# Query-key stacks tiled by kind instead of by token half, and the product with V split only at PSUM banks

## The chip, the cores and the metric

One core of one Trainium2 chip. The time is device microseconds of one execution, median over runs; the kernel is one program launched once, with everything from the first LayerNorm to the last store inside.

## The reference

S = 2048 tokens, D = 640, 32 heads of 20, window W = 256, gMLP width Fh = 864:

```python
def _A_ref(x, wqkv, wo):
    q, k, v = ...                      # (x @ wqkv) as 32 heads of 20
    scores = einsum("bhqd,bhkd->bhqk", q, k) * 20 ** -0.5
    mask = (i - j >= 0) & (i - j < 256)
    p = softmax(where(mask, scores, -1e9))
    return einsum("bhqk,bhkd->bhqd", p, v) ... @ wo

def _B_ref(x, w_in, w_sp, b_sp, w_out):
    z = gelu(x @ w_in)
    z1, z2 = z[..., :Fh], layernorm(z[..., Fh:])
    g = einsum("ts,bsf->btf", w_sp, z2) + b_sp
    return (z1 * g) @ w_out

h = x + _A_ref(layernorm(x), wqkv, wo)
out = h + _B_ref(layernorm(h), w_in, w_sp, b_sp, w_out)
```

## The kernel before

**Stages.** LayerNorm of x and the V projection, then the query and key projections (line 568 to 570), then attention, then the output projection with the residual, then the gMLP. The instruction order of TensorE (PE), VectorE (DVE), ScalarE (ACT) and SyncE (SP) is the order in which the code is written; each of these engines works strictly in that order, and an instruction that waits holds back all behind it on its engine. GpSimd (POOL) is placed by the scheduler.

**Precision by parts.** A query or key is cut into three bf16 parts. A dot product of 20 numbers becomes one matmul of 120 rows: six pairs of parts times 20. Rows 120 to 122 hold, for queries, three parts of minus the row's maximum, and for keys the constant ONES, so that a matmul over 123 rows gives score minus maximum, ready for the exponential.

**Stacks.** Four heads at a time form a stack g (8 stacks). A stack lies in one of three slots, `slot_0`, `slot_1` and the pair `xb`; the next but one is loaded while one is in use. Every slot has two SBUF tiles. Before, tile b holds one half of the tokens (0 to 1023, 1024 to 2047), and in it queries (a = 0) and keys (a = 1) of the four heads. `load_stack` fills it with 24 DMAs (L311) out of the DRAM buffer `qk_d`: for each half of the tokens six pairs of parts, each for queries and for keys. SP issues them in the attention steps, one or two to a step, the first half of the tokens first; the last is issued about at the end of the stack two ahead.

**Steps.** The attention stage is a loop over 128 steps s; step s belongs to stack g = s // 16 and to its block of keys kb = s % 16 of 128 tokens. Each step has four turns hh, one for a head. A turn issues

- `max_item(s + 16, hh)`: the query block one stack ahead against its up to 384 keys, in four matmuls of 32 query rows and 288 keys (L341; while the lead is built up, one matmul of 128 rows, L345), into one of three banks; then the masked row maximum on DVE (L351);
- `score_item(s, hh)`: the key block against up to 384 queries, four matmuls of 32 key rows and 288 queries (L394; in the last 15 steps the sixteen of two heads share a double bank), into one of three other banks; then the exponential on ACT (L397) into `pt`; after the fourth turn POOL puts zeros outside the window;
- at turn 1 and at turn 3 one of the two parts of `pv_item(s - 2)`, the product of V with the 384 exponentials of a key block (L422), four matmuls, one for each head, accumulated into a bank `pv` that stands for 512 queries. A part ends at column 512 where the block crosses a bank; where none ends inside, the 384 columns are cut into 192 and 192.

When an odd block kb is done, 256 queries are complete and are copied out of the bank: the first half of a bank by ACT (L438), the second by DVE; L441 stores them.

**The maxima's way.** After eight query blocks, at turn 1 of the step with (s + 16) % 8 == 0, `max_rows` transposes the 32 columns of maxima (L357), DVE and POOL make three parts, L366 stores them to the DRAM buffer `m_d`, and one step later L368 loads them into rows 120 to 122 of the queries of the right token half. So the second half's maxima of a stack (b = 1) are written in the first steps of that same stack, eight steps before a score needs them.

**Where a matmul's tokens cross from one tile to the other** (at token 1024) `tokens` cuts it into two.

Of the kernel before, what the change touches and what calls it, by code (L numbers as in the profile page):

```python
# [7 lines left out]
F32 = mybir.dt.float32  # L8
F32R = mybir.dt.float32r
BF16 = mybir.dt.bfloat16  # L10
# [5 lines left out]
P = 128  # L16
S = 2048
D = 640
H = 32
DH = 20  # L20
# [8 lines left out]
ONES = 1.0019378662109375  # L29
# [5 lines left out]
def block_kernel(ctx, tc, x, xt, wqk, wv, wo, w_in, wsp, bsp, w_out, out):  # L35
    nc = tc.nc
# [201 lines left out]
    with ExitStack() as ab:  # L238
# [59 lines left out]
        def load_stack(g):  # L298


            st = slot_w[g % 3]
            if g < 3:
                for h in st:
                    nc.gpsimd.memset(h[96:P, 1], ONES)
                    if g == 2:
                        yield
            for b in range(2):
                for j, parts in enumerate(((0, 0), (0, 1), (0, 2), (1, 0), (1, 1), (2, 0))):
                    for a in range(2):
                        src = qk_d[g // 4, parts[a], b, a * DH:(a + 1) * DH, g % 4 * 4:g % 4 * 4 + 4]  # L310
                        nc.sync.dma_start(st[b][j:6 * DH:6, a], src)  # L311
                        yield

        def tokens(st, rows, a, hh, t0, n):

            o = 0
            while o < n:
                c, t = divmod(t0 + o, S // 2)
                w = min(n - o, S // 2 - t)
                yield o, w, st[c][:rows, a, hh, t:t + w]  # L320
                o += w

        def one(st, rows, a, hh, t0, n):
            (_, _, x), = tokens(st, rows, a, hh, t0, n)
            return x

        def max_item(g, qb, hh, strips=True):

            st = slot_ap[g % 3]
            ps = s1_tile()  # L330
            lo = max(0, qb - 2) * P
            n = (qb + 1) * P - lo
            keep = mask[:, 384 - n:]
            if strips:
                skip = 32 if qb > 1 else 0
                if skip:
                    n, keep = 288, strip
                for j in range(4):
                    q0 = qb * P + 32 * j
                    for o, w, k in tokens(st, 120, 1, hh, lo + skip * j, n):  # L340
                        nc.tensor.matmul(ps[32 * j:32 * j + 32, o:o + w], one(st, 120, 0, hh, q0, 32), k,  # L341
                                         start=True, stop=True, tile_position=(0, 32 * j))
            else:
                for o, w, k in tokens(st, 120, 1, hh, lo, n):
                    nc.tensor.matmul(ps[:, o:o + w], one(st, 120, 0, hh, qb * P, P), k, start=True, stop=True)  # L345
            b, c = divmod(qb, 8)
            if c == 0 and hh == 0:
                m_cols[g, b] = tmp2.tile([P, 32], F32, tag="mcol", bufs=2, name=f"mcol{g}_{b}")
            junk = tmp2.tile([P, 384], BF16, tag="junk", bufs=2, name=f"junk{g}_{qb}_{hh}")
            c += hh * 8  # L350
            nc.vector.tensor_tensor_reduce(out=junk[:, :n], in0=ps[:, :n], in1=keep, scale=1.0,  # L351
                                           scalar=NEG, op0=OP.add, op1=OP.max, accum_out=m_cols[g, b][:, c:c + 1])

        def max_rows(g, b):

            ps = s1_tile()[:32, :P]
            nc.tensor.transpose(ps, m_cols.pop((g, b)), ident)  # L357
# [8 lines left out]
            nc.sync.dma_start(rows.rearrange("a r c -> r a c"), m3.bitcast(F32))  # L366
            yield
            nc.sync.dma_start(slot_w[g % 3][b][120:123, 0], rows.rearrange("a (h r) c -> a h (r c)", h=4))  # L368
            yield

        p_tiles, pv_tiles = {}, {}
# [1 line left out]
        def score_item(u, hh):  # L373


            g, kb = divmod(u, NT)
            st = slot_ap[g % 3]
            n = min(384, S - kb * P)
            if hh == 0:
                p_tiles[u] = tmp3.tile([P, 4, 384], F32, tag="pt", bufs=4, name=f"pt{u}")  # L380
            pt = p_tiles[u]
            if u > NU - LEAD:
                if hh % 2 == 0:
                    bank2.append(bank2.pop(0))
                ps = bank2[-1][:, hh % 2]
            else:
                ps = s2_tile()
            for i in range(4):
                k0 = kb * P + 32 * i
                b, e = 32 * i, min(n, 32 * i + 288)  # L390
                if NU - LEAD < u and 4 * (u - NU + LEAD - 1) + hh < 6:
                    b, e = 0, n
                for o, w, q in tokens(st, 123, 0, hh, kb * P + b, e - b):
                    nc.tensor.matmul(ps[32 * i:32 * i + 32, b + o:b + o + w], one(st, 123, 1, hh, k0, 32), q,  # L394
                                     start=True, stop=True, tile_position=(0, 32 * i))
            if u <= NU - LEAD:
                nc.scalar.activation(pt[:, hh, :n], ps[:, :n], AF.Exp, scale=SCALE)  # L397
# [46 lines left out]
        if True:  # L444
# [134 lines left out]
            def split_qk(m, c, ps):  # L579
                sg = tmp.tile([P, 3, 512], BF16, tag="ta", bufs=3, name=f"sg{m}_{c}")  # L580
                rest = tmp.tile([P, 512], F32, tag="tb", bufs=2, name=f"rest{m}_{c}")
                nc.vector.tensor_tensor(out=rest, in0=ps, in1=stds[c], op=OP.mult)
                yield
                nc.scalar.activation(sg[:, 0, :], rest, AF.Copy)
                yield
                (nc.gpsimd if m > 5 else nc.vector).tensor_tensor(out=rest, in0=rest, in1=sg[:, 0, :],
                                                                  op=OP.subtract)
                if (m, c) == (9, 3):
                    nc.gpsimd.tensor_copy(out=sg[:, 1, :], in_=rest)
                else:  # L590
                    nc.scalar.activation(sg[:, 1, :], rest, AF.Copy)
                nc.gpsimd.tensor_tensor(out=sg[:, 2, :], in0=rest, in1=sg[:, 1, :], op=OP.subtract)
                T = S // 4
                base = qk_d[m // 5, 0, c // 2, m % 5 * 8, 0, c % 2 * 256:c % 2 * 256 + 256]
                nc.sync.dma_start(bass.AP(tensor=base.tensor, offset=base.offset,
                                          ap=[[T, P], [2 * 2 * DH * H // 2 * T, 3], [1, 256]]), sg.bitcast(F32))

            halves = [slice(0, HD), slice(HD, D)]
            load_x(0)
# [807 lines left out]
```

## Time and profile before

| | |
|---|---|
| median of 3 runs | 1126.63 us (1126.02 to 1129.81) |
| profiled execution | 1125.76 us, span 1124.0 us |
| mean granted TensorE clock | 0.995 |
| busy, share of the span | PE 97%, weight loads 87%, DVE 67%, ACT 50%, POOL 28% |
| attention steps 0 to 111 | about 239 to 449 us |

PE is busy for 1089.4 us of 1124.0. In the rows below, a line of a timeline gives the start in us, the time in us until the last of the group ends (or of one, for a single instruction), the engine, the code line, the operation and its output and inputs, partitions by free size, and after x the number of instructions; what stands in brackets is the idle time just before and what ended it. Rows of stages give the stretch, its length, then busy time with the number of instructions for PE, weight loads, DVE, ACT and POOL, then the granted clock, the share of DMA engines that are busy and GB/s. SPq is the queue of DMA issues on SP.

### The profile page before, as it was taken

What the parts mean: (1) busy time and instruction counts of PE and PEld (TensorE: products, weight loads), DVE (VectorE), ACT (ScalarE), POOL (GpSimd) and SP (SyncE); (2) the same over time, 40 slices, a digit from 0 to 9 for tenths busy, and PEclk for the clock granted to TensorE, in tenths of its full rate; (3) what the DMA queues carried; (4) which work ended last, traced back from release to release, by engine and by line L of the source; (5) the groups of instructions that cost most, each with busy time, mean ns of one, the idle gap of its engine ahead of it and who ended that gap; (6) DMA issues with size and microseconds to landing.
All of it is one profiled execution on the core that took longest, in us unless ns stands there. A gap on an engine that the chain in (4) does not pass through costs nothing.

```text
span 1124.0 us, 28713 instructions
## 1 busy us (share of the span) xinstructions
PE 1089.4 (97%) x11139; PEld 980.3 (87%) x11139; DVE 752.8 (67%) x2070; ACT 567.5 (50%) x1155; POOL 319.6 (28%) x447
## 2 busy tenths in 40 slices
PE   8999999989999999999999999999999999999998
PEld 8998887657877777699899999999999899999998
DVE  6643444779988999588877678655358974556542
ACT  4444443248988899735566567434347521222210
POOL 4324446766766666723200011000001000000000
PEclk9999999989999999999999999999999999999999
DMA  7834567545555555689554522242251563444321
GB/s 256 283 113 135 171 186 248 183 157 181 179 179 172 177 178 165 170 249 311 218 195 167 182 91 76 75 134 90 104 171 57 180 209 119 124 148 148 98 87 60
DMA packets 87672, 180.57 MB, mean 161 GB/s; under 512 B 11440, under 2 KB 45760, under 8 KB 83648
## 3 DMA queue, kind: packets, MB, share of 16 engines
q1 hardware_dynamic: 87536, 178.74, 49.8%
q8 instruction: 87, 1.43, 0.5%
q14 instruction: 49, 0.40, 0.1%
HBM read 120.82 MB, written 57.88 MB: 159 GB/s over the span
## 4 chain that ended last, share of the span: by engine, by line
PE 72%; DMA 8%; ACT 7%; DVE 6%; issue 3%; POOL 2%; SPq 1%; DVEq 0%; POOLq 0%; ACTq 0%
PE g L1136 22%; PE out_ps L1201 8%; ACT pt L397 5%; PE pv L422 4%; PE zb L1028 4%; PE qk L568 3%; PE qk L569 3%; PE qk L570 3%; PE bank L341 3%; PE bank L394 3%; PE zx L976 2%; PE zv L976 2%; PE zy L976 1%; PE wo_ps L101 1%; DMA o_d<-ot 1%
## 5 line engine op out<-in xcount | busy, mean ns | idle before, releaser
L397 ACT ACTIVATE pt<-bank 128x384 f32<-128x384 f32 (+1 forms) x452 | 180.1, 478 | 26.4 <-PE bank L394 16.2
L803 ACT ACTIVATE aw<-fx 128x512 fp32r<-128x512 f32 (+2 forms) x160 | 93.7, 596 | 173.5 <-PE g L1136 120.7
L1136 PE MATMUL g<-zl,aw 128*128 128x432 f32 x768 | 171.0, 358 | 0.0
L351 DVE CUSTOM_DVE_ANT_0 junk<-bank,strip 128x288 bf16<-128x288 f32 x392 | 156.7, 454 | 16.3 <-PE bank L341 13.8
L1136 PEld LDWEIGHTS g<-zl,aw 128*128 128x128 f32 x768 | 143.6, 188 | 5.9
L422 PE MATMUL pv<-pt,v_sb 128*32 128x192 f32 (+3 forms) x1984 | 129.6, 323 | 6.2 <-ACT ot L438 3.8
L1136 PE MATMUL g<-ze,aw 128*128 128x432 f32 x576 | 134.0, 360 | 0.3 <-DVE row L797 0.2
L797 DVE TENSOR_TENSOR aw<-fx,aw 128x512 fp32r<-128x512 f32 (+2 forms) x160 | 102.7, 647 | 37.1 <-ACT aw L803 35.8
L1136 PEld LDWEIGHTS g<-ze,aw 128*128 128x128 f32 x576 | 107.0, 188 | 6.7 <-ACT aw L803 1.2
L401 POOL TENSOR_SCALAR_AFFINE_SELECT pt<-pt 128x512 f32<-128x512 f32 x128 | 83.9, 656 | 62.7 <-ACT pt L397 60.2
L394 PE MATMUL bank<-slot 123*32 123x288 bf16 (+7 forms) x1296 | 94.4, 276 | 4.9 <-ACT pt L397 3.5
L1201 PE MATMUL out_ps<-wout,y_sp 128*128 128x320 f32 (+1 forms) x630 | 96.2, 309 | 0.4 <-ACT y_sp L140 0.4
L341 PE MATMUL bank<-slot 120*32 120x288 bf16 (+6 forms) x1280 | 92.2, 277 | 3.6 <-issue 1.6
L1028 PE MATMUL zb<-win,aw 128*128 128x432 f32 x480 | 95.4, 359 | 0.0
L1201 PEld LDWEIGHTS out_ps<-wout,y_sp 128*128 128x128 f32 (+1 forms) x630 | 94.1, 188 | 1.2 <-ACT y_sp L140 0.7
L87 POOL TENSOR_TENSOR mvz<-mvz,half 128x1 f32<-128x1 f32 x16 | 10.1, 633 | 298.8 <-DVE mvz L86 296.8
L1028 PEld LDWEIGHTS zb<-win,aw 128*128 128x128 f32 x480 | 89.9, 187 | 5.0 <-ACT row L803 0.3
L422 PEld LDWEIGHTS pv<-pt,v_sb 128*32 128x32 f32 x1984 | 59.9, 110 | 18.1 <-issue 9.9
L797 DVE TENSOR_TENSOR row<-g,row 128x432 f32<-128x432 f32 x80 | 48.2, 604 | 37.8 <-PE g L1136 36.9
L394 PEld LDWEIGHTS <-slot 123*32 123x32 bf16 x1728 | 58.5, 97 | 15.3 <-issue 6.0
L404 POOL TENSOR_SCALAR_AFFINE_SELECT pt<-pt 128x512 f32<-128x512 f32 x112 | 71.4, 637 | 0.0
L351 DVE CUSTOM_DVE_ANT_0 junk<-bank,mask 128x384 bf16<-128x384 f32 (+2 forms) x120 | 51.7, 447 | 21.1 <-PE bank L345 15.8
(196 smaller groups left out, 2247.1 us busy)
## 6 DMA issues: line engine op xcount, KB each, us to landing
slot<-qk_d SPq DMA_DIRECT2D x144, 160.0 KB
fx<-wsp_in SPq DMA_DIRECT2D x32, 512.0 KB
qk_d<-sg SPq DMA_DIRECT2D x40, 384.0 KB
fx<-hn_d SPq DMA_DIRECT2D x32, 320.0 KB
o_d<-ot SPq DMA_DIRECT2D x64, 128.0 KB
xb<-qk_d SPq DMA_DIRECT2D x48, 160.0 KB
z_d<-row SPq DMA_DIRECT2D x16, 432.0 KB
g_d<-row SPq DMA_DIRECT2D x16, 432.0 KB
```

Of the source, the lines that this page charges most:

```text
L341: nc.tensor.matmul(ps[32 * j:32 * j + 32, o:o + w], one(st, 120, 0, hh, q0, 32), k, start=True, stop=True, tile_position=(0, 32 * j))
L351: nc.vector.tensor_tensor_reduce(out=junk[:, :n], in0=ps[:, :n], in1=keep, scale=1.0, scalar=NEG, op0=OP.add, op1=OP.max, accum_out=m_cols ...
L394: nc.tensor.matmul(ps[32 * i:32 * i + 32, b + o:b + o + w], one(st, 123, 1, hh, k0, 32), q, start=True, stop=True, tile_position=(0, 32 * i))
L397: nc.scalar.activation(pt[:, hh, :n], ps[:, :n], AF.Exp, scale=SCALE)
L401: nc.gpsimd.affine_select(out=pt[:, :, :P], in_=pt[:, :, :P], pattern=[[0, 4], [1, P]], base=0, channel_multiplier=-1, compare_op=OP.is_ge ...
L404: nc.gpsimd.affine_select(out=pt[:, :, 256:], in_=pt[:, :, 256:], pattern=[[0, 4], [-1, P]], base=-1, channel_multiplier=1, compare_op=OP. ...
L422: nc.tensor.matmul(ps[32 * hh:32 * hh + 32, a - 512 * c:b - 512 * c], v_sb[:, kb, v0:v0 + 32], pt[:, hh, a - kb * P:b - kb * P], start=fir ...
L797: (eng or nc.vector).tensor_tensor(out=out, in0=a, in1=b, op=op)
L803: nc.scalar.activation(out, a, AF.Copy)
L1028: nc.tensor.matmul(b[0][:, :HF], a[t][:, x, kk], win2[0][:, y, kk, h * HF:(h + 1) * HF], start=kk + x + y == 0, stop=kk == KD - 1 and x == 1)
L1136: nc.tensor.matmul(ps, w[m][:, x, k], zc[k][m][:, y], start=start and k + x + y == 0, stop=stop and k == 3 and x == 1, skip_group_check=True)
L1201: nc.tensor.matmul(ps[j][:, :HD], src[:w, a, k, :], e1["wout"][:w, b, k, j * HD:(j + 1) * HD], start=(k == 0 and a + b == 0), stop=(k == K ...
```

## The change

A slot's two tiles now hold queries (tile 0) and keys (tile 1) of all 2048 tokens, each with rows 120 to 122 for its own. `qk_d` is laid out for it. A load fetches the same 20 rows of 4 heads and half of the tokens as before, and the order of the 24 loads is the same, but their target alternates between the two tiles, and in each it takes 4 pieces of 2 KB to a row instead of one of 8 KB. Every maximum and score is one matmul for each 32 rows, at token 1024 too. And `pv_item` cuts only where a PSUM bank ends: a block that crosses none is one part of 384 columns, issued at turn 1, together with the copy that follows it.

```diff
-    qk_d = dram.tile([2, 3, 2, 2 * DH, H // 2, S // 4], F32, name="qk_d")
+    qk_d = dram.tile([2, 3, 2 * DH, H // 2, S // 2], F32, name="qk_d")
...
-            slot_ap[i] = [h.bitcast(BF16).rearrange("p (a h t) -> p a h t", a=2, h=4) for h in halves]
-            slot_w[i] = [h.bitcast(F32).rearrange("p (a h t) -> p a h t", a=2, h=4) for h in halves]
+            slot_ap[i] = [h.bitcast(BF16).rearrange("p (h t) -> p h t", h=4) for h in halves]
+            slot_w[i] = [h.bitcast(F32).rearrange("p (h t) -> p h t", h=4) for h in halves]
...
         def load_stack(g):
...
-                        src = qk_d[g // 4, parts[a], b, a * DH:(a + 1) * DH, g % 4 * 4:g % 4 * 4 + 4]
-                        nc.sync.dma_start(st[b][j:6 * DH:6, a], src)
+                        t = slice(b * T, (b + 1) * T)
+                        src = qk_d[g // 4, parts[a], a * DH:(a + 1) * DH, g % 4 * 4:g % 4 * 4 + 4, t]
+                        nc.sync.dma_start(st[a][j:6 * DH:6, :, t], src)
                         yield
...
         def max_item(g, qb, hh, strips=True):
...
-                    for o, w, k in tokens(st, 120, 1, hh, lo + skip * j, n):
-                        nc.tensor.matmul(ps[32 * j:32 * j + 32, o:o + w], one(st, 120, 0, hh, q0, 32), k,
-                                         start=True, stop=True, tile_position=(0, 32 * j))
+                    nc.tensor.matmul(ps[32 * j:32 * j + 32, :n], tokens(st, 120, 0, hh, q0, 32),
+                                     tokens(st, 120, 1, hh, lo + skip * j, n),
+                                     start=True, stop=True, tile_position=(0, 32 * j))
...
         def max_rows(g, b):
...
-            nc.sync.dma_start(slot_w[g % 3][b][120:123, 0], rows.rearrange("a (h r) c -> a h (r c)", h=4))
+            t = slice(b * S // 4, (b + 1) * S // 4)
+            nc.sync.dma_start(slot_w[g % 3][0][120:123, :, t], rows.rearrange("a (h r) c -> a h (r c)", h=4))
...
         def pv_item(u):
...
-            mid = (a // 512 + 1) * 512 if a // 512 < (e - 1) // 512 else a + 192
+            mid = min(e, (a // 512 + 1) * 512)
```

The places in the programs of instructions at which something moves or waits for something else. A row is the code line, the operation, its output and inputs, the size, and the semaphores it waits for; DMAHW stands for a transfer that has landed, the engines' names for their work. In the changed kernel L341, L394, L397, L422 and L438 are L331, L385, L389, L414 and L430, and the DMAs L311, L366 and L368 are L312, L357 and L360.

ACT, at step 3 of stack 2 (`pv_0` is the product's bank for the first 512 queries, `ot_0_0` the copy of its first half), before:

```order
L397 ACTIVATE pt_4522<-bank_119 128x384 [waits PE_49,Pool_49]
L397 ACTIVATE pt_4522<-bank_120 128x384 [waits PE_49]
L397 ACTIVATE pt_4522<-bank_121 128x384 [waits PE_49]
L397 ACTIVATE pt_4522<-bank_119 128x384 [waits PE_49]
L438 ACTIVATE ot_0_0_4571<-pv_0_4481 128x256 [waits DMAHW2_49,PE_49]
```

and after:

```order
L389 ACTIVATE pt_4310<-bank_119 128x384 [waits PE_49,Pool_49]
L389 ACTIVATE pt_4310<-bank_120 128x384 [waits PE_49]
L430 ACTIVATE ot_0_0_4331<-pv_0_4273 128x256 [waits DMAHW2_49,PE_49]
L389 ACTIVATE pt_4310<-bank_121 128x384 [waits PE_49]
L389 ACTIVATE pt_4310<-bank_119 128x384 [waits PE_49]
```

The copy has moved from behind the fourth exponential of the step to between the second and the third.

PE, at turn 1 of step 2 of stack 3 (`slot_0_99` and `slot_1_100` are the two tiles of this stack's slot; `pt_5353` and `pt_5049` are the exponentials of block 0), before:

```order
L394 LDWEIGHTS slot_0_99
L394 MATMUL bank_120<-slot_0_99 32x288 [waits Activation_49]
...
L422 MATMUL pv_0_5491<-pt_5353,v_sb 32x192 [waits Pool_49]
L422 MATMUL pv_0_5491<-pt_5353,v_sb 32x192 x3
```

and after:

```order
L385 LDWEIGHTS slot_1_100 [waits DMAHW6_49]
L385 MATMUL bank_120<-slot_0_99,slot_1_100 32x288 [waits Activation_49]
...
L414 MATMUL pv_0_5183<-pt_5049,v_sb 32x384 [waits PE_49,Pool_49]
L414 MATMUL pv_0_5183<-pt_5049,v_sb 32x384 x3
```

The score's first weight load now waits for a transfer, the one that brings the second half's maxima (by the counter's value), and the product is one part of 384.

SP, around that transfer, before:

```order
L366 DMA m_d<-m_3_1_5371 32x3x64 [waits DMAHW2_49,DVE_49,Pool_49]
...
L441 DMA o_d<-ot_3_1_5439 128x256 [waits DMAHW5_49,DVE_49]
L368 DMA slot_1_100<-m_d 3x2048 [waits DMAHW6_49,DMAHW2_49]
L311 DMA xb_94<-qk_d 20x2048 [waits DMAHW7_49]
```

and after:

```order
L357 DMA m_d<-m_3_1_5067 32x3x64 [waits DMAHW2_49,DVE_49,Pool_49]
...
L433 DMA o_d<-ot_3_1_5131 128x256 [waits DMAHW5_49,DVE_49]
L360 DMA slot_0_99<-m_d 3x4x512 [waits DMAHW6_49,DMAHW2_49,PE_49]
L312 DMA xb_95<-qk_d 20x4x512 [waits DMAHW7_49]
```

The load of the maxima goes to the query tile, which PE's scores are reading, and now waits for PE as well, for the last score of step 1.

PE, at the first maximum of stack 4 (`slot_0_1950` and `slot_1_1951` are the tiles of its slot) and at that stack's ninth block of queries, before:

```order
L341 LDWEIGHTS slot_0_1950 [waits DMAHW5_49,DMAHW7_49,DMAHW4_49,DMAHW3_49,DMAHW1_49,DMAHW0_49]
L341 MATMUL bank_118<-slot_0_1950 32x128 [waits DVE_49]
...
L341 LDWEIGHTS slot_1_1951 [waits DMAHW3_49,DMAHW7_49,DMAHW2_49,DMAHW1_49]
L341 MATMUL bank_118<-slot_0_1950,slot_1_1951 32x256 [waits DVE_49]
L341 LDWEIGHTS slot_1_1951 [waits DMAHW7_49,DMAHW5_49]
L341 MATMUL bank_118<-slot_1_1951 32x32 [waits DMAHW2_49]
```

and after, at the first maximum:

```order
L331 LDWEIGHTS slot_0_1950 [waits DMAHW7_49,DMAHW5_49,DMAHW2_49,DMAHW4_49,DMAHW3_49,DMAHW1_49,DMAHW0_49]
L331 MATMUL bank_118<-slot_1_1951,slot_0_1950 32x128 [waits DVE_49]
L331 LDWEIGHTS slot_0_1950
L331 MATMUL bank_118<-slot_1_1951,slot_0_1950 32x128
L331 LDWEIGHTS slot_0_1950
```

The waits that stood at the ninth block, for the loads of the second half of the tokens, now stand at the first; by the counters' values they reach the last of the 24 loads.

More of the change, by code (lines that the diff above doesn't have):

```diff
@@ L298, in load_stack @@
         def load_stack(g):
-            st = slot_w[g % 3]
+            st, T = slot_w[g % 3], S // 4
             if g < 3:
-                for h in st:
-                    nc.gpsimd.memset(h[96:P, 1], ONES)
+                for i in range(2):
+                    nc.gpsimd.memset(st[1][96:P, 2 * i:2 * i + 2], ONES)
                     if g == 2:
@@ L309, in load_stack @@
                     for a in range(2):
-                        src = qk_d[g // 4, parts[a], b, a * DH:(a + 1) * DH, g % 4 * 4:g % 4 * 4 + 4]
-                        nc.sync.dma_start(st[b][j:6 * DH:6, a], src)
+                        t = slice(b * T, (b + 1) * T)
+                        src = qk_d[g // 4, parts[a], a * DH:(a + 1) * DH, g % 4 * 4:g % 4 * 4 + 4, t]
+                        nc.sync.dma_start(st[a][j:6 * DH:6, :, t], src)
                         yield
         def tokens(st, rows, a, hh, t0, n):
[L316 to L325, printed above, removed]
+            return st[a][:rows, hh, t0:t0 + n]
         def max_item(g, qb, hh, strips=True):
@@ L339, in max_item @@
                     q0 = qb * P + 32 * j
-                    for o, w, k in tokens(st, 120, 1, hh, lo + skip * j, n):
-                        nc.tensor.matmul(ps[32 * j:32 * j + 32, o:o + w], one(st, 120, 0, hh, q0, 32), k,
-                                         start=True, stop=True, tile_position=(0, 32 * j))
-            else:
-                for o, w, k in tokens(st, 120, 1, hh, lo, n):
-                    nc.tensor.matmul(ps[:, o:o + w], one(st, 120, 0, hh, qb * P, P), k, start=True, stop=True)
+                    nc.tensor.matmul(ps[32 * j:32 * j + 32, :n], tokens(st, 120, 0, hh, q0, 32),
+                                     tokens(st, 120, 1, hh, lo + skip * j, n),
+                                     start=True, stop=True, tile_position=(0, 32 * j))
+            else:
+                nc.tensor.matmul(ps[:, :n], tokens(st, 120, 0, hh, qb * P, P), tokens(st, 120, 1, hh, lo, n),
+                                 start=True, stop=True)
             b, c = divmod(qb, 8)
@@ L392, in score_item @@
                     b, e = 0, n
-                for o, w, q in tokens(st, 123, 0, hh, kb * P + b, e - b):
-                    nc.tensor.matmul(ps[32 * i:32 * i + 32, b + o:b + o + w], one(st, 123, 1, hh, k0, 32), q,
-                                     start=True, stop=True, tile_position=(0, 32 * i))
+                nc.tensor.matmul(ps[32 * i:32 * i + 32, b:e], tokens(st, 123, 1, hh, k0, 32),
+                                 tokens(st, 123, 0, hh, kb * P + b, e - b),
+                                 start=True, stop=True, tile_position=(0, 32 * i))
             if u <= NU - LEAD:
```

6 lines of the change are left out of this document (3 added, 3 removed).

## Prediction

> **What bounds the kernel now.** I read the page's first lines, the busy times by stage, PE's timeline through one change of stack, and SyncE's timeline beside it.
>
> ```profile
> span 1124.0 us, 28713 instructions
> PE 1089.4 (97%) x11139; PEld 980.3 (87%) x11139; DVE 752.8 (67%) x2070; ACT 567.5 (50%) x1155; POOL 319.6 (28%) x447
> ...
> 239.00:449.00 210.00, 195.00 (x5767) 160.82 (x5758) 188.74 (x955) 183.64 (x477) 141.49 (x242) 0.98 0.56 172
> ```
>
> PE is the bound. The change works in the attention steps; of the 210 us in which seven stacks of 16 steps run, PE shows 195 busy, and DVE (189) and ACT (184) stand close behind. What PE does not do there can be won, but only as far as those two let it; a new wait of PE is lost in full, because nothing else is queued on it.
>
> The change of stack at 390 us (step 80; its first running maximum is L341, its first score L394):
>
> ```profile
> 390.25 0.23 PE L341 MATMUL bank<-slot 120*32 120x128 bf16 x4
> ...
> 390.56 0.31 PE L394 MATMUL bank<-xb 123*32 123x288 bf16 x4
> 390.88 0.28 PE L357 MATMUL bank<-ident,mcol 128*32 128x128 f32 x1
> 391.10 0.53 PE L422 MATMUL pv<-pt,v_sb 128*32 128x192 f32 x8
> ...
> 393.98 0.31 PE L394 MATMUL bank<-xb 123*32 123x288 bf16 x4
> ...
> 388.21 2.20 SPq L311 DMA_DIRECT2D slot<-qk_d  x3
> 392.74 0.32 SPq L366 DMA_DIRECT2D m_d<-m  x1
> 395.47 0.27 SPq L368 DMA_DIRECT2D xb<-m_d  x1
> ```
>
> PE starts the new stack's maxima at 390.25, while the stack's last three loads were issued at 388.2, 388.9 and 389.7: they bring the second half of the tokens, which nobody needs for eight steps. The transposes of the maxima of the running stack's second half are at 390.88; their way to DRAM starts at 392.74, their way back into the stack at 395.47. PE is by then past 393.98, the second score of step 82. Before the change none of this is waited for.
>
> **What the product with V gains.** Durations are start to start, since matmuls overlap.
>
> ```profile
> 399.51 0.43 PE L422 MATMUL pv<-pt,v_sb 128*32 128x128 f32 x8
> 399.73 0.33 PE L341 MATMUL bank<-slot 120*32 120x288 bf16 x4
> ...
> 400.26 0.62 PE L422 MATMUL pv<-pt,v_sb 128*32 128x256 f32 x8
> 400.69 0.29 PE L341 MATMUL bank<-slot 120*32 120x288 bf16 x1
> ...
> 402.05 0.52 PE L422 MATMUL pv<-pt,v_sb 128*32 128x192 f32 x8
> 402.37 0.32 PE L341 MATMUL bank<-slot 120*32 120x288 bf16 x4
> 402.50 0.25 PE L394 MATMUL bank<-xb 123*32 123x96 bf16 x4
> ...
> 402.62 0.31 PE L341 MATMUL bank<-slot 120*32 120x288 bf16 x4
> ```
>
> Parts of 128, 192 and 256 columns take 0.22, 0.32 and 0.43 us: time goes with columns. One part of 384 is 0.43 + 0.21 = 0.64 against 0.65 for two; 72 merged steps (8 stacks, nine steps each) win 72 x 0.01 = 0.7 us. A score split at token 1024 (402.50 to 402.62) takes 0.12, an unsplit maximum (402.37 to 402.50) 0.13: the unsplit scores and maxima, the 488 matmuls fewer that the loops give, win nothing.
>
> The larger gain is a wait. Block 1, 5, 9 or 13 was finished in the second half of its step, its copy stood behind four exponentials, and the next step's product, which writes the same bank, waits for it:
>
> ```profile
> 397.29 0.31 PE L394 MATMUL bank<-xb 123*32 123x288 bf16 x4
> 397.86 0.64 PE L422 MATMUL pv<-pt,v_sb 128*32 128x256 f32 x8 [0.26 <-ACT ot L438]
> ...
> 397.33 0.39 ACT L438 ACTIVATE ot<-pv 128x256 f32<-128x256 f32 x1
> ```
>
> From 397.29, less 0.12 for the score itself, PE stands 0.45 us. Now the product is whole at the step's second score and the copy goes out two exponentials earlier; two exponentials at about 0.4 us each are more than the 0.45. What is late next is the copy itself: it waits about 0.6 us for the longer product, with two exponentials behind it on ACT, which PE covers with the 0.25 us of pairs and the next product. Three such steps in each of seven stacks: 21 x 0.45 = 9.5 us. The fourth (390.56 to 391.10) lies ahead of a wait below and is counted there.
>
> **What the layout adds.** Three waits, all of PE, each with the whole queue of PE behind it, and with it ACT, DVE and POOL, which live on its banks.
>
> *Wait A.* The maxima of a stack now wait for every load of its key tile, the last included. Three loads end at 389.7; how long one takes to land is shown by one row only, a matmul released by a load:
>
> ```profile
> 233.49 2.20 SPq L311 DMA_DIRECT2D slot<-qk_d  x3
> ...
> 238.83 0.24 PE L341 MATMUL bank<-slot 120*32 120x128 bf16 x4 [0.95 <-DMA slot<-qk_d]
> ...
> 267.06 3.59 SPq L311 DMA_DIRECT2D xb<-qk_d  x4
> ...
> 271.74 0.24 PE L341 MATMUL bank<-xb 120*32 120x128 bf16 x3
> ```
>
> The third was issued at 235.0, so 3.8 us. Landed at 389.7 + 3.8 = 393.5, against 390.25: 3.3 us, at steps 32, 48, 64, 80 and 96: 16.5. Stack 2 is loaded earlier in its step group (last issue 269.96, 273.8 against 271.74): 2.0. Sum 18.5.
>
> *Wait B.* The store of the second half's maxima into the query tile now waits for PE's score at the end of step 1 of the stack, and the second score of step 2 waits for its landing. Chain from the transposes: 1.86 to the first DMA (390.88 to 392.74), 2.73 until it has landed (395.47), and the way back, which no row shows; between the shortest and the longest first leg (1.5 and 3.7 us, rows below) I take 2.5, since it is nearest in size. Together 7.1. PE reaches the score 3.10 us after the transposes, 2.7 without the old 0.41 us wait: 4.4 us. I take 4.0, because after wait A the loads are in and the first leg meets an emptier queue, as at 450.71. For six stacks 24; stack 0 and stack 7 from these:
>
> ```profile
> 245.74 0.27 SPq L368 DMA_DIRECT2D slot<-m_d  x1
> 246.21 0.48 PE L394 MATMUL bank<-slot 123*32 123x288 bf16 x4
> ...
> 420.97 0.33 SPq L366 DMA_DIRECT2D m_d<-m  x1
> 424.67 0.27 SPq L368 DMA_DIRECT2D slot<-m_d  x1
> ...
> 450.33 0.87 PE L394 MATMUL pair<-slot 123*32 123x384 bf16 x16
> 450.71 0.32 SPq L366 DMA_DIRECT2D m_d<-m  x1
> 452.21 0.27 SPq L368 DMA_DIRECT2D slot<-m_d  x1
> ```
>
> 245.74 + 2.5 - 246.21 = 2.0; and 452.21 + 2.5 - 451.0 (the row's last quarter) = 3.7. Sum 29.7.
>
> *Wait D.* The first maximum of all waits for stack 0's last load:
>
> ```profile
> 183.29 0.23 PE L345 MATMUL bank<-slot 120*128 120x128 bf16 x1
> ...
> 184.99 2.20 SPq L311 DMA_DIRECT2D slot<-qk_d  x3
> ```
>
> Issued at 186.5, landed at 190.3: 7.0 us, in a stage in which PE runs without a gap.
>
> *The clock.* One long wait of PE is in the trace already, and the clock after it:
>
> ```profile
> 243.48 0.43 PE L394 MATMUL bank<-slot 123*32 123x288 bf16 x4 [3.21 <-ACT pt L397]
> ...
> 236.90:240.30 3.40, 1.97 (x33) 0.76 (x31) 3.33 (x15) 0.63 (x1) 3.26 (x3) 1.00 0.50 176
> 240.40:247.10 6.70, 3.62 (x61) 2.74 (x64) 3.19 (x17) 4.16 (x10) 4.51 (x9) 0.50 0.22 68
> ```
>
> Half speed for 6.7 us, 3.5 of them work. Half of 3.5 is 1.7; some falls into the next wait: 1.5 for each of six B and for D, 10.5 us. After A it costs nothing, since B's chain of DMAs runs meanwhile. The Trainium skill (TensorE: Matmul & The Clock Gate, "What's actually happening") has the clock halve after an idle window of about 3.4 us and windows that run freely. Read strictly, a wait of 4.0 us would rarely cover a whole window and the clock term would be about 2, the sum 47. The row speaks against it: the window before 240.3 still held 1.97 us of matmuls and was followed by half speed; I stay with the row.
>
> The loads' 80 pieces of 2 KB in place of 20 of 8 KB change neither SyncE's time for one (bounds: 0.70 now, and 0.36 for a store of 384 pieces) nor the landing, as far as a row tells:
>
> ```profile
> L311 SPq DMA_DIRECT2D slot<-qk_d x144: 694/702/1885, 160.1 to 418.1; - x144
> 242.94 0.36 SPq L595 DMA_DIRECT2D qk_d<-sg  x1
> ```
>
> **Sum**: 29.7 + 18.5 + 7.0 + 10.5 - 9.5 - 0.7 = 55.5. The profiled execution took 1125.76 us, 0.9 below the median of the runs: 1181.
>
> **Rivals.** (1) The loads and the maxima land early and no wait remains: the 21 + 6 waits go, 27 x 0.45 + 0.7 = 13 us, so 1113. It decides at one point: the way of the maxima there and back would have to be done 2.7 us after the transposes, when the trace starts its first leg only after 1.86. 4%. (2) Landing is quicker: 2.5 us for a load and 1.5 for each leg (the shortest first leg). Then A 5 x 2.0 + 0.7, B 6 x 2.2 + 1.0 + 2.7, D 5.7, clock 3.5, less 10.2: 27, so 1152. The row at 450.71 speaks for it, 420.97 against. 18%. (3) The clock falls only after a wholly idle window: 47, so 1173. 16%. (4) SyncE's issue grows with the pieces: at a quarter of the proportional 2.8 us nothing, at 2.0 us 24 loads are 48 us, a stack has 30 (210 / 7), and 7 x 18 = 126 us come on top: 1252. Against it the 0.36 us row. 5%. (5) The gain and the waits cancel: 2%.
>
> The forecast, 1181, within 1170 to 1200, has 50%; the rest, 5%, lies above it, at legs of 3.7 us and longer half speed. 1150 to 1206 takes in cases 2 and 3 and some of the rest. 0.3% is about what a measurement of this kernel can tell from no change: faster 0.04, within it 0.02, slower 0.94.
>
> **What would show it.** Right: PE waiting for slot<-qk_d at the first maximum of six stacks by 2 to 4 us and once by 7, for slot<-m_d eight times by 2 to 5 us, half clock in that stage, products of 384 columns at 0.64 us, and no wait for ot at L438's successor. Wrong: waits below 2 us, a full clock, or SyncE issues of 2 us.

## The result and the profile after

The changed kernel takes 1211.36 us (median of 6 runs, 1208.88 to 1214.94) against 1129.42 us for the kernel before (6 runs, 1126.02 to 1130.80): ratio 1.0732, 95% interval 1.0708 to 1.0757. It is 82 us slower; 1181 was predicted, with a range to 1206. The direction and the three places of the loss are as predicted, the size is not. The profiled execution took 1214.94 us. From its page and its stages:

```profile
span 1213.2 us, 26529 instructions
PE 1120.3 (92%) x10075; PEld 971.2 (80%) x10075; DVE 758.0 (62%) x2070; ACT 570.3 (47%) x1155; POOL 316.9 (26%) x447
...
183.00:239.00 56.00, 48.69 (x216) 30.88 (x215) 33.30 (x115) 13.14 (x21) 29.48 (x26) 0.94 0.49 165
239.00:529.00 290.00, 229.02 (x4886) 154.79 (x4888) 201.03 (x982) 190.25 (x484) 148.79 (x248) 0.85 0.43 132
```

The attention steps take 290 us instead of 210; PE is busy 229 of them. Its clock is 0.85 in the mean; if it is always either full or half, as in the windows below, that is half speed for 87 us (0.15 x 2 x 290). The waits of PE, who it waited for, total, times, longest:

```profile
PE bank L385 <- DMA slot<-m_d: 15.3, 5, 4.0
PE bank L331 <- DMA xb<-qk_d: 14.4, 3, 5.2
PE bank L331 <- DMA slot<-qk_d: 11.6, 2, 5.9
PE bank L385 <- DMA xb<-m_d: 7.4, 2, 3.7
PE bank L335 <- DMA slot<-qk_d: 7.2, 1, 7.2
PE bank L385 <- ACT pt L389: 4.9, 2, 4.7
PE pair L385 <- DMA slot<-m_d: 4.5, 1, 4.5
PE bank L331 <- DMA o_d<-ot: 4.5, 1, 4.5
```

The three new waits stand there alone at the top. Wait A, at L331, is 14.4 + 11.6 + 4.5 = 30.5 us in six stacks (the last row is the same wait of seven semaphores, put down to the one that came last). Wait B, at L385, is 15.3 + 7.4 + 4.5 = 27.2 us in eight. Wait D, at L335, is 7.2 us, once. No wait for ot is left. The change of stack that answers to the one at 390 us of before, on PE, on SP, and by windows:

```profile
366.99 0.26 PE L385 MATMUL bank<-xb,xb 123*32 123x32 bf16 x4
372.49 0.30 PE L331 MATMUL bank<-slot,slot 120*32 120x128 bf16 x4 [5.24 <-DMA xb<-qk_d]
...
373.30 0.40 PE L348 MATMUL bank<-ident,mcol 128*32 128x128 f32 x1
...
381.17 0.43 PE L385 MATMUL bank<-slot,slot 123*32 123x288 bf16 x4 [3.20 <-DMA slot<-m_d]
381.38 1.50 PE L414 MATMUL pv<-pt,v_sb 128*32 128x384 f32 x8
```

```profile
358.17 0.73 SPq L360 DMA_DIRECT2D slot<-m_d  x1
359.00 0.36 SPq L433 DMA_DIRECT2D o_d<-ot  x1
359.41 2.42 SPq L312 DMA_DIRECT2D slot<-qk_d  x3
361.88 0.48 SPq L433 DMA_DIRECT2D o_d<-ot  x1
362.40 2.96 SPq L312 DMA_DIRECT2D slot<-qk_d  x3
365.46 0.42 SPq L433 DMA_DIRECT2D o_d<-ot  x1
365.94 2.40 SPq L312 DMA_DIRECT2D slot<-qk_d  x3
...
375.26 0.33 SPq L357 DMA_DIRECT2D m_d<-m  x1
375.65 1.60 SPq L312 DMA_DIRECT2D xb<-qk_d  x2
377.35 0.42 SPq L433 DMA_DIRECT2D o_d<-ot  x1
377.88 0.73 SPq L360 DMA_DIRECT2D slot<-m_d  x1
```

```profile
369.72:376.55 6.83, 4.06 (x69) 2.60 (x73) 2.62 (x14) 2.31 (x6) 1.20 (x3) 0.50 0.23 68
376.55:379.96 3.41, 1.19 (x32) 0.72 (x24) 1.86 (x9) 1.56 (x4) 1.94 (x4) 1.00 0.45 133
379.96:386.79 6.83, 5.62 (x68) 2.85 (x72) 2.28 (x10) 2.94 (x7) 1.22 (x2) 0.50 0.25 79
```

The last load of the new stack is issued at about 367.5 (the third of 365.94), just after PE stood still at 367.25 (372.49 less 5.24); SP had been issuing almost without a pause since 358. PE goes on at 372.49, 4.9 us after that issue. The maxima go out at 375.26, come back from 377.88 on, and PE goes on at 381.17, 7.9 us after its transposes. In both waits the clock falls to half (369.72 and 379.96), and it stays there for 6.83 us, past the wait's end.

### The profile page after: what moved, and what is told of

The parts are those of the page before. It is cut to its first block, busy times and chain, and to the rows that moved or that the text cites. A ratio compares the mean times of both kernels' runs of the same rounds, so it can differ in the third digit from the quotient of the medians.

```text
span 1213.2 us, 26529 instructions
## 1 busy us (share of the span) xinstructions
PE 1120.3 (92%) x10075; PEld 971.2 (80%) x10075; DVE 758.0 (62%) x2070; ACT 570.3 (47%) x1155; POOL 316.9 (26%) x447
## 4 chain that ended last, share of the span: by engine, by line
PE 41%; DMA 6%; DVE 4%; ACT 2%; issue 1%; SPq 1%; POOL 1%; DVEq 0%; POOLq 0%; ACTq 0%
PE g L1128 20%; PE out_ps L1193 8%; PE zb L1020 4%; PE zx L968 2%; PE zv L968 2%; PE zy L968 1%; DMA rs<-r_d 1%; PE zw L968 1%; PE yt_ps L1182 1%; DMA fx<-wsp_in 1%; PE wo_ps L101 1%; DMA inv<-o_d 1%; DVE zl L789 1%; DMA wraw<-w_in_in 1%; DVE row L789 1%
## 5 line engine op out<-in xcount | busy, mean ns | idle before, releaser
L389 ACT ACTIVATE pt<-bank 128x384 f32<-128x384 f32 (+1 forms) x452 | 180.6, 475 | 85.9 <-PE bank L385 44.8
L414 PE MATMUL pv<-pt,v_sb 128*32 128x384 f32 (+2 forms) x1408 | 124.3, 428 | 2.1 <-POOL pt L396 1.5
L331 PE MATMUL bank<-slot,slot 120*32 120x288 bf16 (+2 forms) x1280 | 95.9, 306 | 23.6 <-DMA slot<-qk_d 11.6
L385 PE MATMUL bank<-slot,slot 123*32 123x288 bf16 (+5 forms) x1296 | 97.9, 309 | 20.2 <-DMA slot<-m_d 15.3
L385 PEld LDWEIGHTS <-slot 123*32 123x32 bf16 x1536 | 52.9, 105 | 52.9 <-issue 25.8
L87 POOL TENSOR_TENSOR mvz<-mvz,half 128x1 f32<-128x1 f32 x16 | 10.2, 637 | 298.4 <-DVE mvz L86 296.4
L331 PEld LDWEIGHTS <-slot 120*32 120x32 bf16 x1280 | 44.1, 105 | 47.5 <-issue 30.3
```

What stands on the lines that cost most here:

```text
L331: nc.tensor.matmul(ps[32 * j:32 * j + 32, :n], tokens(st, 120, 0, hh, q0, 32), tokens(st, 120, 1, hh, lo + skip * j, n), start=True, stop= ...
L385: nc.tensor.matmul(ps[32 * i:32 * i + 32, b:e], tokens(st, 123, 1, hh, k0, 32), tokens(st, 123, 0, hh, kb * P + b, e - b), start=True, sto ...
L414: nc.tensor.matmul(ps[32 * hh:32 * hh + 32, a - 512 * c:b - 512 * c], v_sb[:, kb, v0:v0 + 32], pt[:, hh, a - kb * P:b - kb * P], start=fir ...
```

## The experiments

In the copies the names and lines of the changed kernel hold up to a shift of a few lines. All ratios are against the kernel before on the same chip. A difference in us between two changed kernels can carry up to 3 us of difference between chips: the kernel before took 1126.24 to 1129.42 us in the five series.

**Which part.** The new cut of the product alone, in the old layout, and the new layout alone:

```diff
-            mid = (a // 512 + 1) * 512 if a // 512 < (e - 1) // 512 else a + 192
+            mid = min(e, (a // 512 + 1) * 512)
```

> The old layout with the new cut of the product with V alone, against the kernel before (1129 us). By the prediction's term C the waits for the copy go and are a clear gain: 21 x 0.45 + 0.7 = 10 us, 1119. By what the changed kernel's trace shows in the steps without a DMA wait (four steps 6.85 us where the four before took 7.12, ideal 6.6), DVE and ACT take over as the bound, and the gain is half of that: 4 to 6 us, 1124. If the copy's wait only moves elsewhere: 1129. The trace then shows four steps in about 6.85 us, and no wait for ot.

> The new layout with the old cut of the product, against the changed kernel (1211 us). If layout and product add up, the waits for slot<-qk_d and slot<-m_d stay as they are (together about 65 us) and the product's 4 to 6 us come back: 1216. If the layout's waits already hid the waits for the copy, the two are one: 1211.

The cut alone: 1126.69 against 1126.24 us, ratio 0.9994 (0.9979 to 1.0009). Neither 10 nor 5 us are won. The layout alone: 1209.82 us, ratio 1.0738 (1.0713 to 1.0763), the same as with the cut. So the layout makes the whole loss, and the cut as good as nothing.

**Wait A alone and wait B alone.**

```diff
-            for _ in range(1 + s % 2 if s >= NT else 2 * min(s, 1)):
+            for _ in range(2 * min(s, 1)):
                 next(ld, None)
```

> The changed kernel with two loads of a stack in each step instead of one or two, so that the last is issued some three steps before the first maximum. Theory (loss = waits A, B, D and half clock after each): wait A, 6 times 5.1 us, goes, and with it 12 us of half clock after it; wait B grows by 1 to 1.5 us each, because PE reaches the second score of step 2 sooner at full speed: 1211 - 30.5 - 12 + 8 = 1177. Rival 1, the clock term is much smaller than read: 1211 - 30.5 + 3 = 1184 or more. Rival 2, SP's queue is full and A comes back in another place: over 1195.

```diff
-            nc.sync.dma_start(slot_w[g % 3][0][120:123, :, t], rows.rearrange("a (h r) c -> a h (r c)", h=4))
+            for h in range(4):
+                src = rows[:, 8 * h:8 * h + 8].rearrange("a r c -> a (r c)")
+                nc.sync.dma_start(slot_w[g % 3][0][120:123, h, t], src)
```

> The changed kernel with the load of the maxima cut into four, one for each head, so that each writes a stretch of the query tile that no score of the first six steps reads. Theory: wait B goes, 27 us, and the half clock after it, some 18 us; SP issues six more DMAs in a stack, which makes wait A up to 1 or 2 us longer, 6 to 12 us: 1211 - 45 + 9 = 1175. Rival 1, B is the time until the maxima themselves land and not the overlap of the regions: no change, 1211. Rival 2, without clock term: 1211 - 27 + 9 = 1193.

Loads earlier: 1189.75 us, 22 less, not 34. Its waits of PE show a 4.6 and a 2.0 us remainder of A, so A is some 24 us shorter, and B has grown from 27.2 to 30.0. These two account for 21 of the 22 us; nothing is left that half speed after A would have cost.

```profile
PE bank L385 <- DMA slot<-m_d: 16.7, 5, 5.0
PE bank L385 <- DMA xb<-m_d: 8.4, 2, 4.4
...
PE pair L385 <- DMA slot<-m_d: 4.9, 1, 4.9
```

Maxima by heads: 1175.98 us, 35 less, as expected; no wait for m_d of B's kind is left, A has grown to 36.5. The waits make 21 of the 35 (27.2 less 6.0), which leaves some 14 for half speed after B, where 18 were expected: the number was met with both terms smaller, and that was luck. So B is indeed a matter of regions that touch: the same maxima, written head by head, hold up nobody. What one wait loses the other takes up in part.

**Both.**

> The changed kernel with both edits, two loads in each step and the load of the maxima by heads. Theory: waits A and B with their half clock go, wait D (7.2 us and 1.9 of half clock) stays, and the A wait of stack 2 stays (4.6 us and about 2 of half clock), since its loads are issued in the first stack's steps behind SP's own waits: 1126 + 9 + 7 + a few us of a full SP queue = 1145, within 1138 to 1155. If the time goes in something else of the layout (splits, pieces, the matmuls' reads): over 1160.

1161.75 us: 17 over the value and 7 over the end of what was expected, in the range of the rival, that the time goes in something else of the layout. The trace shows wait A in its place: 22.1 + 7.0 + 1.1 = 30.2 us at L331, although two loads stood in each step. PE at a change of stack, SP before it, and SP's own waits for the maxima:

```profile
356.07 0.30 PE L331 MATMUL bank<-slot,slot 120*32 120x128 bf16 x4 [5.29 <-DMA o_d<-ot]
```

```profile
342.63 1.91 SPq L312 DMA_DIRECT2D slot<-qk_d  x2
346.96 1.20 SPq L362 DMA_DIRECT2D slot<-m_d  x4
348.26 0.35 SPq L435 DMA_DIRECT2D o_d<-ot  x1
348.65 3.17 SPq L312 DMA_DIRECT2D slot<-qk_d  x4
```

```profile
SPq L362 <- DMA m_d<-m: 13.7, 10, 2.4
```

From 344.5 to 346.96 SP stands and waits until the first half's maxima have landed in DRAM, with the last loads behind it. That named a second cause of A: not the table of one or two loads to a step alone, but SP's queue. The standing is 2.4 of these 5.29 us; the rest is the landing of loads that are issued as PE arrives.

**Mended.** From that: whole rows, so that a stack takes 12 loads; the store of the maxima one step later, their load by heads and two steps later, so that SP finds both done.

```diff
-            for b in range(2):
+            for b in range(2 if g < 2 else 1):
...
-                        t = slice(b * T, (b + 1) * T)
+                        t = slice(b * T, (b + 1) * T) if g < 2 else slice(0, 2 * T)
...
+            yield
             rows = m_d[g, b]
...
-            for _ in range(1 + s % 2 if s >= NT else 2 * min(s, 1)):
+            for _ in range(1 if s >= NT else 2 * min(s, 1)):
...
-                if hh == 3 and u1 % 8 == 1 and s <= NU - LEAD + 1:
+                if hh == 3 and u1 % 8 in (1, 3) and s <= NU - LEAD + 3:
```

> The changed kernel with what the new layout allows: 12 loads of whole rows in a stack, one to a step, in place of 24; the load of the maxima by heads, two steps later, and the store of the maxima one step later, so that SP does not stand and wait for either with loads queued behind. Theory: waits A and B were made by SP's queue and by regions that touch; both are gone, and only wait D (7.2 us, some 2 of half clock) is left: 1126 + 9 = 1136, 1132 to 1141. If the layout has a price of its own (pieces, transfers, the matmuls' reads): over 1145.

1136.54 us, ratio 1.0093 (1.0068 to 1.0118): on the number. Half as many loads and the later places came in one run, so it is not shown how much each of them is worth. Of the waits for `qk_d` only D and one of 1.5 us are left, of those for `m_d` 2.6 us in three:

```profile
PE bank L335 <- DMA slot<-qk_d: 7.1, 1, 7.1
...
PE bank L388 <- DMA slot<-m_d: 2.0, 2, 1.2
...
PE bank L331 <- DMA slot<-qk_d: 1.5, 1, 1.5
```

Then wait D, by ten more groups of projections ahead of the first maximum:

```diff
-            for n in range(20):
+            for n in range(30):
                 next(dense, None)
```

> The run before it with ten more groups of the last projections ahead of the first maximum, 7 us of PE work, so that the last load of stack 0 has landed; ten maxima at the end of the lead then have no projection beside them. Theory: D goes too, a maximum alone costs some 0.1 us for DVE: 1128, 1124 to 1132, no slower than the kernel before. Rival: the work is only moved, and PE waits for DVE at the lead's end what it won: 1134 or more.

1125.10 us, ratio 0.9979 (0.9963 to 0.9995), with D at 1.1 us. So nothing near 82 us belongs to the layout as such; the loss was in the waits that its schedule made, and in half speed behind them. This version is just faster than the kernel before, by 0.05 to 0.37%; with the old cut of the product it is just slower (below). The longer lead was not tried in the old layout.

**The clock.** PE is given work in the waits, which are left as they are:

```diff
+        def fill(ps, n):
+            one = ident.bitcast(BF16)
+            for _ in range(n):
+                nc.tensor.matmul(ps[:32, :256], one[:, :32], one, start=True, stop=True)
...
+            if (qb, hh) == (0, 0) and g != 1:
+                fill(ps, 44 if g else 60)
...
+            if (kb, hh) == (2, 1):
+                fill(ps, 44)
```

> The changed kernel, its waits untouched, with PE kept busy in them: matmuls of 256 bf16 columns whose result is overwritten stand ahead of the first maximum of stacks 2 to 7 (44 of them, about 4.7 us), ahead of the second score of step 2 of every stack (44) and ahead of the very first maximum (60). They take no time from the program where they fit into the wait. Theory: the clock stays full behind A, B and D; half clock lost 35 us in the changed kernel's trace, of which some 9 after A are not won, since B's way of the maxima runs meanwhile and B gets longer; the rest, about 24 us, is won: 1211 - 24 = 1187 (1183 to 1195). Rival (the prediction's term): 10 us, 1201. If the half clock costs nothing beside the waits: 1211 or a little more.

1202.03 us, ratio 1.0664 (1.0643 to 1.0686), mean clock 0.993: 8 to 9 us won, near the rival's number, not the theory's 24. The rows say why (L321 is the filling, L338 the maxima, L394 the scores):

```profile
360.66 4.97 PE L321 MATMUL bank<-ident 128*32 128x256 bf16 x44
367.27 0.24 PE L338 MATMUL bank<-slot,slot 120*32 120x128 bf16 x4 [1.64 <-DMA o_d<-ot]
...
370.95 4.75 PE L321 MATMUL bank<-ident 128*32 128x256 bf16 x42
375.48 0.30 PE L394 MATMUL bank<-slot,slot 123*32 123x288 bf16 x3
```

From the first maximum to the released score it is 8.2 us (367.27 to 375.48), and 8.7 in the changed kernel (372.49 to 381.17). The way of the maxima sets this stretch; at full speed PE only waits longer in it. Half speed between A and B is nearly free, and what comes after B is paid.

But 8 to 9 us is a least value, because the filling did not fit into every wait. Stack 0 in the changed kernel, from the issue of the load of the maxima to the score, and the same with filling:

```profile
257.18 0.74 SPq L360 DMA_DIRECT2D slot<-m_d  x1
...
259.95 0.43 PE L385 MATMUL bank<-slot,slot 123*32 123x288 bf16 x4 [2.11 <-DMA slot<-m_d]
```

```profile
255.38 0.74 SPq L367 DMA_DIRECT2D slot<-m_d  x1
255.81 6.25 PE L321 MATMUL bank<-ident 128*32 128x256 bf16 x42
261.79 0.30 PE L394 MATMUL bank<-slot,slot 123*32 123x288 bf16 x3
```

2.8 us have become 6.4, and in stack 6 3.1 (497.44 to 500.50) have become 4.3 (485.98 to 490.31): there the filling ends last, not the load, and costs some 5 us by itself. With these put back, half speed is worth 13 to 14 us, an estimate that agrees with the 14 of the maxima by heads.

**Where the cut's gain went.** First DVE: its maximum over half of the columns, with the old and with the new cut.

```diff
-            nc.vector.tensor_tensor_reduce(out=junk[:, :n], in0=ps[:, :n], in1=keep, scale=1.0,
+            w = n // 2 if strips and qb > 1 else n
+            nc.vector.tensor_tensor_reduce(out=junk[:, :w], in0=ps[:, n - w:n], in1=keep[:, n - w:n], scale=1.0,
```

> The kernel before with DVE's row maximum over the last 144 of the 288 columns only (part of the maximum is left out), which takes some 0.15 us of 0.38 from each of DVE's steps. It is the base for the next run. If the wait for the copy is what PE's steps end on, this changes little: 1124 to 1126. If DVE paces the steps (26.7 us busy of 28.1 in a stack): 1115 to 1120.

> The new cut of the product in the old layout, with the same shortened maximum. Theory: DVE was what took the product's gain, so with DVE out of the way the waits for the copy count again and this is 6 to 10 us below the run before it, at about 1110. Rival: the gain went into the order of PE and ACT over their three banks, and it is within 2 us of the run before it.

1126.43 (ratio 0.9993, 0.9973 to 1.0013) and 1123.91 (0.9967, 0.9950 to 0.9984): 2.5 us between them, so DVE had taken at most a quarter of the 10. Two more with the place of the copy and of the second part:

> The old layout with the new cut of the product, the copy of block 1, 5 or 9 moved behind the third exponential of its step instead of the second. Theory: what took the gain is the one long product, 0.65 us without a score, in which ACT runs dry (0.2 us idle in each such step of the run with the new cut alone), not the copy's place: no gain, 1125 to 1127. Rival: the copy stood too early and held back the exponentials behind it: 1120.

> The old layout and the old cut, the second part of each product at turn 2 instead of turn 3. The block is complete one turn earlier, the copy stands ahead of the fourth exponential, and no product is longer than 0.43 us. If the wait for the copy is worth its 0.45 us once ACT does not run dry: 21 x 0.4 = 8 us, 1118 to 1121. If PE's and ACT's exchange over the three banks sets 28 us for a stack whatever the copy does: 1125 to 1127.

1130.71 (1.0026, 1.0011 to 1.0040) and 1126.02 (0.9993, 0.9971 to 1.0016): nothing is won by either, and the copy moved later is 0.1 to 0.4% slower. Then four banks for the scores and two for the maxima, with the short maximum, and in the mended layout:

```diff
-        ring = {1: banks[2::-1], 2: banks[3:]}
+        ring = {1: banks[1::-1], 2: banks[2:]}
```

> The old layout and the old cut, with the shortened maximum of the run of that name (part of the maximum left out) and two banks for the maxima and four for the scores in place of three and three. Base for the next run. The wait for the copy stays, since the copy still stands behind four exponentials: 1123 to 1127.

> The same with the new cut of the product. Theory: with three banks ACT runs dry during the long product and PE waits for it in the next step; with a fourth bank of scores ahead, ACT has work, PE does not wait, and the copy's 0.45 us are won at last: 8 us or more below the run before it, about 1115. Rival: within 3 us of it; then it is not the exchange of PE and ACT over the banks that took the gain.

> The mended new layout (12 loads, maxima by heads, longer lead) with four banks for the scores and two for the maxima, nothing left out. If the bank for the scores is worth more than the one for the maxima, under 1120; since DVE is busy 26.8 us of a stack's 28, two banks for it should cost as much as four for ACT give: 1123 to 1130.

1132.00 (1.0042, 1.0024 to 1.0060), 1132.89 (1.0056, 1.0034 to 1.0078) and 1154.12 (1.0252, 1.0227 to 1.0277). The new cut gains nothing over the old. That does not clear the banks for the scores, since the base is itself 5 us over what was expected of it: two banks for the maxima may be a limit of their own and hide a gain. In the full kernel the exchange of one bank loses 29 us (1154.12 - 1125.10), where 1123 to 1130 was expected; PE then waits 61 times for DVE's maximum (14.0 us), and 6 times (1.1 us) with three banks. Last, the cut in the mended layout:

> The mended new layout with the old cut of the product: what the new cut is worth where no DMA wait covers it. From the run with the cut alone (ratio 0.999) no difference: 1125 to 1127, as the mended layout with the new cut.

1129.82, ratio 1.0032 (1.0016 to 1.0049), against 0.9979 with the new cut: there it is worth some 5 us, not nothing as expected.

What the cut does in the old layout shows in the stacks. From the first maximum of one stack to that of the next, the kernel before took 28.9, 30.5, 30.0, 29.2 and 28.1 us (271.74 to 418.35), and with the cut alone it is 28.1, 28.2, 28.2, 28.8 and 28.3 (271.83 to 413.32). The fastest of before and its waits, then one with the cut alone:

```profile
390.25:418.35 28.10, 27.44 (x834) 23.23 (x831) 26.73 (x137) 26.12 (x69) 19.74 (x34) 1.00 0.60 178
```

```profile
PE bank L394 <- issue: 3.8, 3, 2.3
PE pv L422 <- ACT ot L438: 3.8, 14, 0.3
...
PE bank L341 <- issue: 1.9, 2, 1.6
```

```profile
328.10:356.26 28.16, 27.91 (x764) 20.34 (x756) 26.80 (x136) 25.84 (x69) 19.67 (x34) 1.00 0.59 180
```

With the cut, two kinds of waits are gone from the list. The waits for the copy were 14, with 3.8 us of idle time in all. But against the stack of 28.10 us the stacks with the cut are no shorter, so PE's time at the copy was not lost time: without it PE (27.91), DVE (26.80) and ACT (25.84) still need 28 us for a stack, and no one of them has more than 2.4 us free. Which of them sets the rate is open. That it is ACT can be argued, since PE waits for it at the banks, but it is the least busy of the three, and its exponential was not shortened in any run.

The other kind are waits that the profile puts down to nothing but issue, 5.9 us in all in the attention steps of before. They are about what its other four stacks have over 28.1 us each (6.1 us together). So the attention stage gets shorter in three of four pairs: the output projection starts at 467.0 us with the cut alone instead of 470.6, with the short maximum at 465.1 instead of 468.0, in the mended layout at 467.3 instead of 474.4; with four banks for the scores it is the other way, 476.8 instead of 472.6. In the old layout the medians of the whole kernel do not show this gain. Each of these starts is from one execution, and the stages behind, which no edit touches, took 651 to 662 us in the profiled executions, 653 in that of the kernel before and 658 in that of the cut alone.

## Why the prediction was wrong, step by step

- **Direction, places and mechanism: right.** Three waits, eight times for m_d, six and once for qk_d, were predicted and are there, and an issue of SP takes 0.8 us, not 2. Wait D was given 7.0 and has 7.2. With the waits mended the time is that of before to within 0.4%.
- **Wait A, 18.5 given, 30.5 measured: the step that failed most.** It took before's time of the last issue (389.7, 0.55 us ahead of PE) and 3.8 us for landing. In the changed kernel SP has more to issue: its loads take 0.8 us each (2.40 for three) in place of 0.73, the load of the maxima 0.73 in place of 0.27. SP's standing for the maxima's landing is not new (11 waits, 12.6 us before; 6 waits, 5.9 us after). In all six stacks the last issue comes between 0.2 us ahead of PE's arrival and 1.5 us after it, and PE goes on 4.3 to 4.9 us after that issue (365.94 and its third; 372.49). I called the 2 KB pieces free "as far as a row tells"; for the small transfer they were not, and I did not add up SP's queue. Which part of the longer landing comes from the pieces and which from the fuller queue was not tried.
- **Wait B, 29.7 given, 27.2 measured**, but part of it was covered by half clock: with PE at full speed the eight stretches, filling included, are 38.9 us (4.5 to 6.0 each), which is more than the waits, since the filling overran some. From the transposes to the released score I summed 7.1 us; it is 7.9 at 372 us (7.7 with a full clock). The way back, which no row showed and I put at 2.5, is 3.3 here (377.88 to 381.17) and 2.8 to 4.1 over the eight.
- **The clock, 10.5 given: near.** At least 8 to 9 by the run with the waits filled, 13 to 14 by the two estimates above, and it was right that half speed after A costs next to nothing. The count of half-speed time alone, some 24 us net, which I set against it after the result, was further off. The rule of the Trainium skill (TensorE: Matmul & The Clock Gate, "What's actually happening") that the clock halves after an idle window of some 3.4 us fits in the window's length (6.83 and 3.41 us above), not in the word idle: the window 376.55 to 379.96 held 1.19 us of matmuls and half speed followed.
- **The product's gain, 10.2 given; by the medians 0 in the old layout and in the changed kernel, 5 in the mended one: wrong.** The step that failed is the price of the wait, 21 x 0.45 us, on the ground that "two exponentials at about 0.4 us each are more than the 0.45". The copy did go ahead and its waits are gone, but a stack takes 28.16 us, where the fastest of before took 28.10. The list of waits had 3.8 us for the copy, not 9.5, and the first rows of the prediction had DVE at 189 and ACT at 184 of 210 us; the text said that the gain goes "only as far as those two let it", but the sum did not use that. What attention did win came from the waits put down to issue, which the prediction does not name.
- **In sum**: a loss of 55.5 us was given and 82 was measured, 26 more. A was 12 too low, the product 10 too high a gain. The other 4 lie in B and the clock together: 40.2 given, 44 by what A and D leave of the 82. These two can't be told apart closer, since a shorter A makes a longer B (loads earlier) and the other way round (maxima by heads). The rest of the 30 us between 1181 and 1211 is the base: the sum was put on 1125.76, and the kernel before has a median of 1129.42 in the result.

## What to carry to other kernels

When a tile is cut another way, ask of each transfer what else the new region touches, and put every wait that this makes to the queue that issues it: a DMA queue in strict order that is full, or that stands for a landing, makes every later load late. A wait of PE is not worth its length where the other engines of the loop are nearly full: here PE, DVE and ACT were busy 26 to 28 us of a stack's 28, and the waits for the copy, taken away, won nothing. Read their busy time over one turn of the loop first. Where a chain of transfers sets a stretch, half clock inside it is nearly free; a wait filled with work shows what the rest costs, if the filling ends before the wait does.

## What the runs showed of the hardware

- The issue of a load of 20 rows took 0.70 us in the median before (160 KB, one piece to a row), 0.77 in the changed kernel (160 KB, four pieces to a row) and 0.70 for 320 KB in whole rows (into `xb` in the mended kernel). The 3-row load of the maxima took 0.27 as 3 rows of one piece, 0.73 as 3 rows of four, and 0.27 again as each of four of its own.
- PE's waits that the profile puts down to nothing but issue are 5.9 us in the kernel before and 8.2 in the mended layout with the old cut, none with the new cut alone and none in the mended layout with the new cut. But the cut alone does not decide it: the new layout with the old cut has none, and the filled run, with the new cut, has 2.4. The 5 us of the cut in the mended layout may be these; what makes them was not tried. The Trainium skill (Runtime: NRT & Kernel Launch, "Instruction fetch mechanics") says that an engine fetches its program in blocks by a DMA queue of its own, mostly hidden; whether that is it, no run here shows.
